# A delta-rule attention layer and two MLPs on one core: the second triangular solve, the K Kᵀ products of chunks 4 and 5 and the loads of chunk 2 take other places in chunks 0 to 3

## The chip, the cores and the metric

The kernel is one program on one core of a Trainium2 chip. The metric is the device time of one execution in microseconds (us). Engines are named as in the profile: PE is TensorE (matmuls), PEld its weight load, DVE is VectorE, ACT is ScalarE, POOL is GpSimd, SP is SyncE, which here only issues DMAs. L454 is line 454 of the kernel before. In the changed kernel the lines behind 364 are two higher, those behind 900 about as much again, and the text says which one is meant where it matters.

## The reference, cut to what matters

```
def _attn_ref(q, k, v, beta):                       # 4 x 8 heads, 768 steps, 48 features
    k_n = k / (np.linalg.norm(k, axis=-1, keepdims=True) + 1e-06)
    for t in range(S):
        y[:, :, t] = einsum('bhd,bhde->bhe', q[:, :, t], state)
        v_old = einsum('bhde,bhd->bhe', state, k_n[:, :, t])
        state = state + beta[:, :, t] * outer(k_n[:, :, t], v[:, :, t] - v_old)

x = y as (3072 tokens, 384)
h = np.maximum(x @ w_in, 0.0);  x = h * h @ w_out                         # 384 -> 2048 -> 384
h = max(x @ w1, x @ w2, x @ w3);  out = h @ w_out2                         # 384 -> 768 -> 384
```

All of it is float32. The kernel splits each float32 operand of the large matmuls in a high and a low part and adds three products.

## The kernel before, in words

**Chunks.** The 768 steps are cut into 12 chunks of 64. Inside a chunk the recurrence is a triangular system, so per chunk the kernel needs three things that do not depend on the state: the products K Kᵀ and K Qᵀ of all 32 heads (`kkps`, matmuls at L180, copied out by ACT at L197 and masked by DVE at L198, and stored to DRAM by `kk_store` and L205), the inverse of the triangular matrix (`solve32`), and the loads of keys, values and inverse (`load_x`, `load_att`). The chunks are handled in pairs, `HALVED[g]` being chunks 2g and 2g+1.

**The solve.** `solve32(g)` inverts for both chunks of a pair at once. `start32` loads the blocks of K Kᵀ into `M32` (a piece of the tile `buf`). `ready` (`prep`, `weighted`, `strict`, L217 to L238) turns them into a scaled triangular matrix, and `solve` (L278) does 30 elimination steps of two dependent DVE instructions each (a product at L283, a sum at L285), which grow from 30 to 240 columns and shrink again, and then one scaling of 1024 columns (L286). `finish32` stores the inverse to `xt_d` (L323). `load_x(c)` reads it back as `xb` (L342) and `x1` (L350), together with a block of K Kᵀ, `k21` (L339).

**Attention of a chunk.** `attention(c)` is a generator of seven stages: `st0` (L436 to L449: scales `v`, multiplies keys and queries with the state `Sb` into `pA` and `pY`, and subtracts `pA` from `v`), `zz` (`merged`: DVE transposes `x1` into `xT` at L404, PE makes `pZ` at L411, ACT copies it out at L412), `ww` (PE makes `pW` at L420 from `xT` and the copy, ACT copies it into `xb`), `mm_u` (`pU`, L464), `st2` (`pY` and `pD`, L514 and L492, and the new state, L499), `st3` (transposes at L532 into the high and low parts `xh` and `xl`, L535 and L536). All these small products share one PSUM pool of two buffers, `ps_at`: `pk`, `pq`, `pA`, `pZ`, `pW`, `pU`, `pD`, `pt` and `pT` take turns in it, and each waits until the one two before it has been read.

**The MLP of a chunk.** `moe_a(c)` multiplies the 256 tokens of a chunk with `w_in` (L572, 18 matmuls per piece `s1`), squares the positive part on ACT (L578 to L580, `gh`), makes the low part `gl` on DVE (L581), and multiplies with `w_out` into `px` (L592, 12 matmuls per piece `s2`, two pieces behind). At its end DVE transposes `px` (L612). There are 8 pieces of each kind in a chunk. In chunk 1 (`halves`) every piece is cut into two steps.

**What sets the order.** While chunk c's MLP runs, `steps` calls other generators in between: `attention(c+1)`, the solve of a later pair, the K Kᵀ of a pair, and in chunk 0 the rest of the weight words (`weights`, `words`, `turn`: L103 to L128). A list of numbers says after which step of the MLP a generator goes one yield further, `True` behind it that what is left over stays for later. The instructions of an engine run in the order in which they were recorded, except that the scheduler moves some, DMA issues above all, ahead. `behind` (L269) orders an instruction after another. In chunk 0 the last word loads of `w_out` (L93) go out on SP, and the keys of chunk 2 (`kq`, L364) on POOL.

**The schedule of before around the change** (L895 to L931). The second solve (pair 1: chunks 2 and 3) does 10 yields in chunk 0 and the rest in the first part of chunk 1. The K Kᵀ of chunks 4 and 5 stands in steps 14 to 24 of chunk 1, between the stages of `attention(2)`. The third solve (pair 2) runs through chunk 2.

Of the kernel before, what the change touches and what calls it, by code (L numbers as in the profile page):

```python
# [39 lines left out]
def delta_moe(ctx, tc, kc, ab, kt, vt, beta, beta32, beta16, kq, w_in, w_out, w1, w2, w3, w_out2, out):  # L40
    nc = tc.nc
# [117 lines left out]
    def two(d, c, p):  # L159

        return d[:, c, 2 * p:2 * p + 2]
# [196 lines left out]
    def load_att(c, p):  # L358
        ds = []
        us = slice(U2 * p, U2 * p + U2)  # L360
        kq_ = None
        if c:
            kq_ = att.tile([R2, U2, 2, C], F32, name="kq", tag="kq")
            ds.append(pool.dma_start(kq_, two(kc, c, p).rearrange("p b q t s -> p (b q) t s")))  # L364
        v = att.tile([128, U2, D], F32, name="v", tag="v")
        ds.append(pool.dma_start(v, two(vt, c, p).rearrange("p b q d -> p (b q) d")))
        pt_ = masked.pop((c, p), None)
        if pt_ is None:
            pt_ = att.tile([128, U2, C], F32, name="p", tag="p")
            ds.append(pool.dma_start(pt_, p_d[c][:, us]))  # L370
        kt_ = ktp[p]
        ds.append(pool.dma_start(kt_[:, 0:U2 * D], two(kt, c, p).rearrange("p b q d -> p (b q d)")))
        for i in x_after:
            for d in ds:
                behind(d.ins, i)
        tiles[c, p] = [kq_, v, xb[:, us], pt_, kt_, None, None, None, None]
# [5 lines left out]
    def attention(c):  # L382
# [158 lines left out]
        both = lambda f: ((f, 0), (f, 1))  # L541
        if c:
            order = ((load, 0),), both(st0), ((merged, 0),), *(((),) if c == 1 else ()), ((ww, 0),), both(mm_u), both(st2), both(st3)
            if c == 2:
                order = order[1], order[0], *order[2:]
        else:
            load(0)
            load_att(c, 0)
            load_att(c, 1)
            order = both(st0), ((merged, 0),), ((ww, 0),), both(mm_u), both(st2), both(st3), both(state)  # L550
# [154 lines left out]
    if True:  # L705
# [19 lines left out]
        def solve32(g, load=(nc.sync, nc.sync), store=((nc.sync,) * 2,) * 2, landing=0):  # L725
# [9 lines left out]
            for n, i in enumerate(solve(vec, M, 32, 64 * len(HALVED[g]), a, tmp32)):  # L735
                for j in solve_after:
                    behind(i.ins, j)
                ops.append(i.ins)
                if g and n == (24 if g == 1 else 8):
                    norm(nm)  # L740
                yield
            finish32(g, M, store)
# [152 lines left out]
        for c in range(NC):  # L895
            extra = []
            if c == 0:
                solve_next = solve32(1, (pool,) * 2)
                extra += [(11 / 15.0, later(3, attention(1))), (list(range(17)), weights(2, 2)), (4.0, later(20, part(solve_next, 10)))]
            elif c == 1:  # L900
                pinned.update({first_matmul.ins.engine: None, last_gl[0].engine: None})
                first_solve = [0] * 3 + [1 + n * 13 // 20 for n in range(20)]
                extra += [(first_solve, solve_next), ([15, 17, 24, 26, 28, 30, 31], attention(2))]
                ahead_[2] = solve32(2, landing=1)
                extra += [([14, 15, 19, 20, 21, 22, 23, 24], kkps(HALVED[2], (at,))), ([26, 32], ahead_[2], True)]
                solve_after[:] = last_vec
                kc_after[:] = raws[-1:]
                prep_after.clear()
            elif c + 1 < NC:
                extra.append(([1, 2, 5 + c // 9, 7 + c // 9, 10, 12, 14] if c % 2 else [1, 2, 4, 6, 8, 11, 13], attention(c + 1)))  # L910
            if c == 2:
                kc_after.clear()
                solve_after.clear()
            if c in ahead_:
                extra.append(([1 + n * 14 // 32 for n in range(32)], ahead_[c]))
            if c > 1 and c in KK:
                extra.append(([3, 4, 4, 5, 6, 7, 8, 9], kkps(HALVED[KK[c]], (at,))))
# [128 lines left out]
```

## Time and profile before

| | before |
|---|---|
| median of 3 runs | 926.25 us (925.52 to 926.77) |
| the profiled execution | 926.38 us, its span 924.4 us |
| PE busy | 868.5 us (94%) |
| DVE busy | 475.8 us (51%) |
| ACT, POOL busy | 376.0 us (41%), 146.6 us (16%) |
| DMA | 98.82 MB, mean 107 GB/s |

The profiled execution takes 2 us more than its span, which is what lies before the first and behind the last instruction. PE is busy nearly all the time, but a share of 94% is a mean: in the slices of the page the first eighth of the span has PE at half and the clock of TensorE below its full value, and from the tenth of the span on there are nines. So the stages must be read apart: where the long chains begin and end, what PE waits for in each, and how fast its clock ran there. A wait of PE is told with what ended it; where the profile says "issue", PE waited for nothing that it shows.

### The profile page before, as it was taken

What the parts mean: (1) busy time and instruction counts of PE and PEld (TensorE: products, weight loads), DVE (VectorE), ACT (ScalarE), POOL (GpSimd) and SP (SyncE); (2) the same over time, 40 slices, a digit from 0 to 9 for tenths busy, and PEclk for the clock granted to TensorE, in tenths of its full rate; (3) what the DMA queues carried; (4) which work ended last, traced back from release to release, by engine and by line L of the source; (5) the groups of instructions that cost most, each with busy time, mean ns of one, the idle gap of its engine ahead of it and who ended that gap; (6) DMA issues with size and microseconds to landing.
All of it is one profiled execution on the core that took longest, in us unless ns stands there. A gap on an engine that the chain in (4) does not pass through costs nothing.

```text
span 924.4 us, 26481 instructions
## 1 busy us (share of the span) xinstructions
PE 868.5 (94%) x11422; PEld 843.0 (91%) x11422; DVE 475.8 (51%) x1068; ACT 376.0 (41%) x799; POOL 146.6 (16%) x241
## 2 busy tenths in 40 slices
PE   5439899899999999999999999999999999999998
PEld 5328888799999999999999999999999999999998
DVE  2978886288348734873586364457232322323221
ACT  1447853353445344544453556564121221212111
POOL 2323121411331133122313300002000000000000
PEclk8557999899999999999999999999999999999999
DMA  9987634732852284337434551334110101000000
GB/s 196 309 256 226 202 83 133 194 96 67 207 160 66 85 215 133 78 87 190 104 82 104 143 146 53 102 107 136 38 37 31 35 18 43 10 26 9 18 18 35
DMA packets 122596, 98.82 MB, mean 107 GB/s; under 512 B 77440, under 2 KB 102832, under 8 KB 122480
## 3 DMA queue, kind: packets, MB, share of 16 engines
q1 hardware_dynamic: 101824, 58.42, 24.1%
q0 software_dynamic: 11584, 32.22, 12.2%
q10 hardware_dynamic: 9072, 6.49, 2.4%
q8 instruction: 90, 1.47, 0.7%
q14 instruction: 26, 0.21, 0.1%
HBM read 72.45 MB, written 24.64 MB: 105 GB/s over the span
## 4 chain that ended last, share of the span: by engine, by line
PE 84%; DVE 8%; DMA 3%; ACT 2%; issue 1%; ACTq 0%; SPq 0%; DVEq 0%
PE p L954 24%; PE px L592 21%; PE p L572 20%; PE po L971 8%; PE pY L514 2%; PE pU L464 2%; DVE buf L283 2%; DVE buf L285 2%; PE pk L180 1%; PE pW L420 1%; DMA kct<-in_kc_dram 1%; PE pZ L411 1%; PE pA L445 1%; DMA raw<-in_moe_w_out_dram 1%; DVE gl L581 1%
## 5 line engine op out<-in xcount | busy, mean ns | idle before, releaser
L954 PE MATMUL p<-x_h,w 128*128 128x384 f32 x864 | 220.1, 336 | 0.0
L592 PE MATMUL px<-wout,gh 128*128 128x384 f32 x768 | 200.6, 342 | 0.4 <-ACT gh L580 0.4
L572 PE MATMUL p<-xh,win_h 128*128 128x256 f32 x576 | 169.6, 294 | 2.0 <-DVE gl L581 1.4
L572 PE MATMUL p<-xl,win_h 128*128 128x256 f32 x576 | 164.0, 285 | 0.3 <-DVE xl L536 0.3
L572 PE MATMUL p<-xh,win_l 128*128 128x256 f32 x576 | 164.0, 285 | 0.0
L954 PEld LDWEIGHTS p<-x_h,w 128*128 128x128 f32 x864 | 156.2, 188 | 0.0
L954 PE MATMUL p<-x_l,w 128*128 128x384 f32 x432 | 145.2, 336 | 0.0
L581 DVE TENSOR_TENSOR gl<-p,gh 128x512 fp32r<-128x512 f32 x96 | 66.2, 690 | 144.8 <-ACT gh L580 144.5
L592 PEld LDWEIGHTS px<-wout,gh 128*128 128x128 f32 x768 | 135.6, 190 | 1.9 <-ACT gh L580 0.6
L592 PE MATMUL px<-wout,gl 128*128 128x384 f32 x384 | 129.6, 337 | 0.0
L578 ACT ACTIVATE p<-p 128x512 f32<-128x512 f32 x96 | 55.9, 582 | 176.0 <-PE p L572 176.0
L572 PEld LDWEIGHTS p<-xh,win_h 128*128 128x128 f32 x576 | 111.0, 193 | 5.3 <-DVE gl L581 1.9
L572 PEld LDWEIGHTS p<-xl,win_h 128*128 128x128 f32 x576 | 111.1, 193 | 0.6 <-DVE xl L536 0.5
L572 PEld LDWEIGHTS p<-xh,win_l 128*128 128x128 f32 x576 | 111.4, 193 | 0.0
L960 DVE TENSOR_TENSOR mx<-p,mx 128x384 f32<-128x384 f32 x48 | 26.7, 557 | 126.7 <-PE p L954 126.6
L954 PEld LDWEIGHTS p<-x_l,w 128*128 128x128 f32 x432 | 81.2, 188 | 0.0
L962 ACT CAST hh<-mx 128x384 fp32r<-128x384 f32 x48 | 24.6, 513 | 125.8 <-DVE mx L961 125.8
L592 PEld LDWEIGHTS px<-wout,gl 128*128 128x128 f32 x384 | 72.7, 189 | 0.0
L285 DVE TENSOR_TENSOR buf<-buf 128x30 f32<-128x30 f32 (+9 forms) x180 | 61.1, 339 | 6.1
L283 DVE TENSOR_TENSOR buf<-buf 128x30 f32<-128x30 f32 (+9 forms) x180 | 60.6, 337 | 5.0
L580 ACT CAST gh<-p 128x512 fp32r<-128x512 f32 x96 | 56.4, 587 | 2.6
L579 ACT ACTIVATE p<-p 128x512 f32<-128x512 f32 x96 | 55.9, 583 | 2.6
(166 smaller groups left out, 1290.7 us busy)
## 6 DMA issues: line engine op xcount, KB each, us to landing
kq<-in_kc_dram POOLq DMA_DIRECT2D x22, 448.0 KB, 5.3
raw<-in_moe_w_dram SPq DMA_DIRECT2D x18, 384.0 KB, 3.5
raw<-in_moe_w_out_dram SPq DMA_DIRECT2D x16, 384.0 KB, 4.4
p<-p POOLq DMA_DIRECT2D x22, 256.0 KB, 3.6
rawp<-in_moe_w_in_dram SPq DMA_DIRECT2D x12, 384.0 KB, 10.3
v<-in_vt_dram POOLq DMA_DIRECT2D x24, 192.0 KB, 3.0
ktp<-in_kt_dram POOLq DMA_DIRECT2D x24, 192.0 KB, 3.6
x<-xs SPq DMA_DIRECT2D x48, 96.0 KB, 3.2
```

The lines of the kernel that those rows point to most:

```text
L283: eng.tensor_tensor(out=tv, in0=M[:, 0:j, j].unsqueeze(2).broadcast_to([u, j, m]), in1=M[:, j, j + 1:n].unsqueeze(1).broadcast_to([u, j, m ...
L285: yield eng.tensor_tensor(out=M[:, 0:j, j + 1:n], in0=M[:, 0:j, j + 1:n], in1=tv, op=ALU.add)
L572: pe.matmul(p1[:, j], w[:, k, f], x[c][:, k], start=n == 0 and j == 0, stop=n == 8, skip_group_check=True)
L578: act.activation(out=p1, in_=p1, func=AF.Relu)
L579: act.activation(out=p1, in_=p1, func=AF.Square)
L580: last_gh[0] = act.copy(gh, p1).ins
L581: last_gl[0] = vec.tensor_sub(out=gl, in0=p1, in1=gh.bitcast(F32)).ins
L592: g = pe.matmul(px[:, h, 0:DM], x[:, j, hs], w, start=f == 0 and i == 0, stop=f == NF - 1 and i == 2, skip_group_check=True)
L954: pe.matmul(p, w[i][:, k, fs], x[:, k], start=n == 0, stop=n == 8)
L960: vec.tensor_max(out=t, in0=ps[1], in1=t)
L962: act.copy(hh[:, f], t2)
L971: pe.matmul(po[:, 0:DM], x[:, f, js], w[:, f], start=i == 0, stop=i == 17)
```

## The change

- The keys of chunk 2 (`kq`) are loaded on SP's queue instead of POOL's, ordered behind the last word load of `w_out`.
- `attention(4)` starts with `st0` and then loads its inverse, as `attention(2)` did already. The norms of pair 2 are made after 4 solve steps instead of 8.
- The second solve does one yield at step 4 of chunk 0 (its preparation) and 14 at steps 7 to 16, and has 18 yields left for chunk 1. Its store for chunk 2 goes half on SP and half on POOL.
- In chunk 1, `attention(2)` has its places one or two half steps later, and the K Kᵀ of chunks 4 and 5 stands at steps 27 to 32, the end of the chunk.
- The third solve does 28 yields in chunk 2 (the last 26 from step 5 on) and 6 at the start of chunk 3. `attention(4)` has later places in chunk 3.

```diff
@@ load_att
         if c:
             kq_ = att.tile([R2, U2, 2, C], F32, name="kq", tag="kq")
-            ds.append(pool.dma_start(kq_, two(kc, c, p).rearrange("p b q t s -> p (b q) t s")))
+            ds.append((nc.sync if c == 2 else pool).dma_start(kq_, two(kc, c, p).rearrange("p b q t s -> p (b q) t s")))
+            if c == 2:
+                behind(ds[-1].ins, raws[-1])
@@ attention
-            if c == 2:
+            if c in (2, 4):
                 order = order[1], order[0], *order[2:]
@@ solve32
-                if g and n == (24 if g == 1 else 8):
+                if g and n == {1: 24, 2: 4}.get(g, 8):
                     norm(nm)
@@ the loop over the chunks
             if c == 0:
-                solve_next = solve32(1, (pool,) * 2)
-                extra += [(11 / 15.0, later(3, attention(1))), (list(range(17)), weights(2, 2)), (4.0, later(20, part(solve_next, 10)))]
+                solve_next = solve32(1, (pool,) * 2, ((nc.sync, pool), (nc.sync,) * 2))
+                extra += [(11 / 15.0, later(3, attention(1))), (list(range(17)), weights(2, 2)), ([4] + [7 + n * 10 // 14 for n in range(14)], solve_next, True)]
             elif c == 1:
                 pinned.update({first_matmul.ins.engine: None, last_gl[0].engine: None})
-                first_solve = [0] * 3 + [1 + n * 13 // 20 for n in range(20)]
-                extra += [(first_solve, solve_next), ([15, 17, 24, 26, 28, 30, 31], attention(2))]
+                first_solve = [0] * 3 + [1 + n * 11 // 15 for n in range(15)]
+                extra += [(first_solve, solve_next), ([16, 17, 24, 26, 28, 30, 32], attention(2))]
+                extra += [([27, 28, 29, 30, 31, 32, 32, 32], kkps(HALVED[2], (at,)))]
                 ahead_[2] = solve32(2, landing=1)
-                extra += [([14, 15, 19, 20, 21, 22, 23, 24], kkps(HALVED[2], (at,))), ([26, 32], ahead_[2], True)]
...
             elif c + 1 < NC:
-                extra.append(([1, 2, 5 + c // 9, 7 + c // 9, 10, 12, 14] if c % 2 else [1, 2, 4, 6, 8, 11, 13], attention(c + 1)))
+                places = [2, 4, 7, 8, 10, 12, 14] if c == 3 else [1, 2, 5 + c // 9, 7 + c // 9, 10, 12, 14] if c % 2 else [1, 2, 4, 6, 8, 11, 13]
+                extra.append((places, attention(c + 1)))
...
-            if c in ahead_:
+            if c == 2:
+                extra.append(([1, 4] + [5 + n * 12 // 26 for n in range(26)], ahead_[c], True))
+            elif c == 3:
+                extra.append(([0, 1, 1, 2, 2, 2], ahead_[2]))
+            elif c in ahead_:
                 extra.append(([1 + n * 14 // 32 for n in range(32)], ahead_[c]))
```

What this does to the order, at three places. First SP's queue in chunk 0 (`raw` are word loads of `w_out`, `kq` and the loads into `buf` and `big` are keys), before:

```order
L93 DMA buf<-in_moe_w_out_dram 128x768
L93 DMA raw<-in_moe_w_out_dram 128x768 x4
L167 DMA buf<-in_kc_dram 112x1024
L167 DMA big<-in_kc_dram 112x1024
L299 DMA b_2366<-in_beta_dram 64x32 x2
```

and now:

```order
L93 DMA raw<-in_moe_w_out_dram 128x768 x4
L364 DMA kq<-in_kc_dram 112x1024
L167 DMA buf<-in_kc_dram 112x1024
L364 DMA kq<-in_kc_dram 112x1024
L167 DMA big<-in_kc_dram 112x1024
L299 DMA b_2591<-in_beta_dram 64x32 x2
```

The four word loads now have four key loads behind them on one queue, where there were two, with two more on POOL's queue.

Second, DVE at the end of chunk 0, from the steps of the second solve to the low part `xl` that chunk 1's first matmuls read, before:

```order
L285 TENSOR_TENSOR buf<-buf 128x9x22
L283 TENSOR_TENSOR buf<-buf 128x210
L499 TENSOR_TENSOR Sb<-pD,Sb 128x384 x2
L612 STREAM_TRANSPOSE xs<-px 128x384 x2
L536 TENSOR_TENSOR xl<-pT,xh 128x3x128 x2
```

and now (L501, L614 and L538 are L499, L612 and L536 of before):

```order
L285 TENSOR_TENSOR buf<-buf 128x12x19
L501 TENSOR_TENSOR Sb<-pD,Sb 128x384
L283 TENSOR_TENSOR buf<-buf 128x234
L285 TENSOR_TENSOR buf<-buf 128x13x18
L283 TENSOR_TENSOR buf<-buf 128x238
L285 TENSOR_TENSOR buf<-buf 128x14x17
L283 TENSOR_TENSOR buf<-buf 128x240
L501 TENSOR_TENSOR Sb<-pD,Sb 128x384
L614 STREAM_TRANSPOSE xs<-px 128x384 x2
L538 TENSOR_TENSOR xl<-pT,xh 128x3x128 x2
```

Ten more solve instructions (from the sum with 10x21 columns to the product with 240) stand ahead of the transposes, five of them between the two updates of the state `Sb`, which free the two PSUM buffers that the transposes at L532 need.

Third, DVE in chunk 1, from the end of the second solve (L286) to the end of the chunk (`pq` is one K Qᵀ block each), before:

```order
L286 TENSOR_TENSOR buf<-buf,a_1183 128x1024
L581 TENSOR_TENSOR gl<-p_1902,gh 128x512
L198 TENSOR_TENSOR buf<-pq,mask 128x512
L436 TENSOR_TENSOR v<-v,normT 128x384
L449 TENSOR_TENSOR v<-v,pA 128x384
L436 TENSOR_TENSOR v<-v,normT 128x384
L449 TENSOR_TENSOR v<-v,pA 128x384
L581 TENSOR_TENSOR gl<-p_2059,gh 128x512
L198 TENSOR_TENSOR big<-pq,mask 128x512
L198 TENSOR_TENSOR buf<-pq,mask 128x512
L581 TENSOR_TENSOR gl<-p_2149,gh 128x512
L198 TENSOR_TENSOR big<-pq,mask 128x512
```

and now, from the transposition `xT` on, which in before stands behind the last of these rows:

```order
L406 STREAM_TRANSPOSE xT<-x_2028 128x256
L583 TENSOR_TENSOR gl<-p_2139,gh 128x512
L198 TENSOR_TENSOR buf<-pq,mask 128x512
L476 COPY u<-pU 128x288
L476 COPY u<-pY 64x96 x2
L198 TENSOR_TENSOR big<-pq,mask 128x512
L501 TENSOR_TENSOR Sb<-pD,Sb 128x384 x2
L526 COPY yy<-pY 64x4x48 x4
L198 TENSOR_TENSOR buf<-pq,mask 128x512
L614 STREAM_TRANSPOSE xs<-px 128x384 x2
L538 TENSOR_TENSOR xl<-pT,xh 128x3x128 x2
L198 TENSOR_TENSOR big<-pq,mask 128x512
```

The four K Kᵀ blocks of PE moved along: they stood ahead of `pZ`, and now stand one each between `pW`, `pU`, `pY`/`pD`, `pT` and the first matmuls of chunk 2.

## Rows read from the trace of the kernel before

**Rows 1.** The page, part 2: TensorE's clock in 40 slices, tenths of full.
```profile
PEclk8557999899999999999999999999999999999999
```

**Rows 2.** The chain that ended last: start us, length us, what.
```profile
129.63 0.92 DVE xl L536 x2
130.59 2.19 PE p L572 x16
...
230.03 4.32 PE p L572 x36
...
278.27 4.30 PE p L572 x36
...
320.48 4.32 PE p L572 x36
```

**Rows 3.** Timeline of PE, first main matmul of chunk 2: start us, length us.
```profile
187.04 0.28 PE L572 MATMUL p<-xh,win_h 128*128 128x256 f32 x1
```

**Rows 4.** PE's waits in chunk 0, then chunks 1 and 2: us, times, longest us.
```profile
PE pZ L411 <- DVE v L449: 3.1, 1, 3.1
...
PE pW L420 <- issue: 3.0, 1, 3.0
PE pA L445 <- DVE buf L198: 1.1, 1, 1.1
PE p L572 <- DVE gl L581: 0.9, 2, 0.5
PE pT L532 <- DVE yy L524: 0.7, 1, 0.7
```

**Rows 5.** Windows behind two waits: us, engines' busy us (count), PEclk, DMA share, GB/s.
```profile
172.40:177.40 5.00, 4.96 (x43) 4.46 (x45) 0.69 (x1) 2.04 (x5) 1.29 (x2) 0.50 0.71 201
109.20:113.00 3.80, 3.75 (x77) 3.68 (x78) 3.80 (x10) 3.26 (x7) 0.00 (x0) 0.58 0.03 13
```

**Rows 6.** DVE's timeline, chunk 0's end to chunk 3: start us, length, [idle before, ended by].
```profile
108.38 0.36 DVE L116 TENSOR_SCALAR raw<-raw 128x384 int32<-128x384 int32 x1 [2.12 <-DMA raw<-in_moe_w_out_dram]
...
128.58 1.05 DVE L612 STREAM_TRANSPOSE xs<-px 128x384 f32<-128x384 f32 x2 [2.41 <-PE px L592]
...
130.46 0.35 DVE L285 TENSOR_TENSOR buf<-buf 128x210 f32<-128x210 f32 x1
...
133.87 0.41 DVE L285 TENSOR_TENSOR buf<-buf 128x238 f32<-128x238 f32 x1
...
148.57 1.22 DVE L286 TENSOR_TENSOR buf<-buf,a 128x1024 f32<-128x1024 f32 x1
...
188.21 0.15 DVE L247 COPY ss<-buf 128x32 f32<-128x32 f32 x1
...
228.20 1.22 DVE L286 TENSOR_TENSOR buf<-buf,a 128x1024 f32<-128x1024 f32 x1
...
234.07 0.69 DVE L581 TENSOR_TENSOR gl<-p,gh 128x512 fp32r<-128x512 f32 x1 [2.95 <-ACT gh L580]
```

**Rows 7.** Timelines of POOL and SP: DMA issues, start us, length us.
```profile
99.29 0.55 POOL L364 DMA_DIRECT2D kq<-in_kc_dram  x1 [2.90 <-PE pY L445]
...
100.09 0.33 SPq L93 DMA_DIRECT2D raw<-in_moe_w_out_dram  x1
...
158.25 0.66 POOL L342 DMA_DIRECT2D xb<-xt  x1 [0.70 <-issue]
```

**Rows 8.** DMA issues of 95 to 101 us: KB each, median us to landing.
```profile
raw<-in_moe_w_out_dram SPq DMA_DIRECT2D x4, 384.0 KB, 5.6
...
big<-in_kc_dram SPq DMA_DIRECT2D x1, 448.0 KB, 9.9
```

**Rows 9.** DMA issues of 100 to 190 us.
```profile
xb<-xt POOLq DMA_DIRECT2D x6, 64.0 KB, 3.2
```

**Rows 10.** DMA queues of 170 to 171 us: packets, MB, share of 16 engines.
```profile
q8 instruction: 1, 0.02, 6.0%
```

**Rows 11.** The chain of 90 to 200 us: start us, length us.
```profile
100.09 8.27 DMA raw<-in_moe_w_out_dram
```

## The prediction, made before the changed kernel was run

> **What bounds the kernel now.** I read the clock line first: from the tenth slice of 23 us on it is full, so what can be won lies in the first quarter [rows 1]. Then the chain of waits, for the places where PE begins 36 main matmuls in a row: these are chunk starts. Chunk 1's main matmuls run from 130.59 us behind the DVE part `xl`, chunk 3 starts at 230.03, chunk 4 at 278.27, chunk 5 at 320.48 [rows 2]; chunk 2, from the timeline, at 187.04 [rows 3]. So chunk 1 takes 56.45 us, chunk 2 42.99, chunk 3 48.24 and chunk 4 42.21. An odd chunk holds the K Kᵀ of a pair, an even one does not, so chunk 3 and chunk 4 are the measure: chunk 1 is 8.2 us too long, chunk 2 0.8.
>
> PE's waits name most of it: in chunk 1, 3.0 before `pW` for nothing that the profile shows, 1.1 before `pA` for a masked block, 0.7 before `pT`, and one of 0.5 before a main piece, 5.3 together; in chunk 0, 3.1 before `pZ` [rows 4]. Each of the two long ones has a tail: the five us behind the first ran at clock 0.50, the 3.8 behind the second at 0.58 [rows 5], where the 1.1 before `pA` left the clock full. The lower level is 1.2 of 2.4 GHz, so the first tail lost 2.5 us and the second 1.6.
>
> What held `pZ` in chunk 0: `pZ` takes the PSUM buffer of `pA`, which DVE frees by the subtraction L449; DVE stood 2.12 us in front of a word operation until 108.38 [rows 6], because the last word load, issued at 100.09 [rows 7], took 8.27 us [rows 11]. Key loads were around it, on POOL's queue from 99.29 [rows 7] and on SP's behind it, the last of which took 9.9 [rows 8].
>
> **The change part by part.** The work of PE is the same, so I sum what each chunk start moves.
>
> *Chunk 0, -0.6.* In before DVE goes from 108.38 to the end of `xl` at 130.55 (129.63 + 0.92) in 22.17 us, of which 2.41 wait for PE's last `px` [rows 2, 6]: 19.76 of work. Ten solve instructions come on top; nine of them took from 130.46 to 134.28 in before [rows 6], so ten cost 4.2. Five short preparation steps move ahead of the landing and one word operation behind it; these I count as equal. That is 24.0 us from the landing to `xl`. The word load now goes out some 0.3 later, behind two short operations, and has all four key loads behind it instead of one ahead and two behind. I take the median of the four word loads, 5.6 us [rows 8]: landing at 106.0, `xl` at 130.0, against 130.55. Bounds: DVE itself cannot be there before about 105.5 (108.38 less its 2.12 of idle, less what it waits for earlier word loads), so -1.1; if the word load takes the longest of these loads, 9.9, it lands at 110.3 and the term is +3.7. The point is that DVE, not PE, now ends chunk 0: what PE gains at `pZ` is hidden.
>
> The Trainium skill ("DMA: Bandwidth & Descriptors", section "Queues, rings and completion order") says that each DMA engine takes the descriptors of one ring in order and goes round robin between rings. By that the four key loads on the same ring cannot delay the words, and the term is -1.1. The trace agrees only in part: with two key loads behind it on its own queue and one beside it the word load took 8.27 us.
>
> *Clock behind it, +1.6.* PE does not wait long at `pZ` any more: DVE passes two word operations, one reciprocal and the subtraction, some 2 us, behind the landing, so `pZ` starts near 108.1, and PE comes there 0.8 later than before, having seven more main matmuls of 0.12 us (4.32 for 36) to do first. Without the tail of 1.6 us PE ends its `px` some 3.6 us earlier, about 125, and the second buffer for `pT` comes free 2 us before `xl` ends, about 128. So a wait of 3 us goes from `pZ` to the end of the chunk. The two rows with a 3 us wait both show a fall of the clock, the 1.1 us one does not [rows 4, 5]; I take the fall, with the price of the shorter tail. Bounds 0 and 2.5.
>
> *Chunk 1, -5.9.* Here the solve has 16 steps left instead of 21, so its scaling, 18.0 us behind the chunk's start in before (148.57 [rows 6]), comes four to five us earlier, and the inverse goes out on two queues. `attention(2)` runs without the K Kᵀ between `st0` and `pZ`. The wait before `pA` goes, since no block of K Kᵀ holds the PSUM in front of it. The 3.0 before `pW`: PE stopped within the 64 matmuls of `pW`, with its operands there, and in that time the queue "instruction" moved one packet of 0.02 MB [rows 10]. So PE waited for its own code, behind the loads of K Kᵀ for the third solve and the stores. Now `pW` has only main pieces ahead of it and no store of K Kᵀ beside it; I take this wait and its tail as gone. The 0.5 before a main piece stays, being a matter of ACT and DVE behind the first piece. At the chunk's end PE finds no `px` to do between `pT` and the next chunk as it did in before: the fourth K Kᵀ block needs both PSUM buffers of `pT`, read by `xl`, which stands behind two transposes of `px`: 1.05 and 0.92 us [rows 2, 6] less six small transposes of 0.1 each, 1.4. Sum: 56.45 - 5.3 - 2.5 + 0.5 + 1.4 = 50.55. Bounds: 48.2, chunk 3's length, and 56.45 if the code waits elsewhere.
>
> *Chunk 2, -0.5.* Its order on PE stays; it had 0.8 us over chunk 4. Its solve starts later: in before the first copy of `ss` came 1.2 us into the chunk (188.21 [rows 6]), now behind `xT`, some 11 us into it, since the last K Kᵀ block is stored only at the chunk's start. This costs DVE, not PE. Bounds -0.8 and +1.5.
>
> *Chunk 3, +1.2.* The solve took from 188.21 to 229.4, 41 us, most of it DVE's own work [rows 6]; 10 us later it ends some 10 to 11 us into chunk 3. The last six yields stand there in front of and around the subtraction that the first K Kᵀ block waits for. DVE had 2.95 us of idle there [rows 6], which covers most of the five steps before it; I count 0.5. The last load of the inverse was issued 8.5 us behind the end of the scaling in chunk 1 (149.79 to 158.25 [rows 6, 7]) and takes 3.2 us [rows 9], 11.7 in all; PE reaches `pZ` some 11 us behind the scaling now: 0.7. Bounds 0 and 3.4, the 2.95 uncovered and more.
>
> Later chunks keep their order. Sum: -0.6 + 1.6 - 5.9 - 0.5 + 1.2 = -4.2. The profiled execution took 926.38, which is 0.13 above the median; so 922.2 against it, and 922.0 as a median.
>
> **The rivals.** *Better (918.8).* The words land as early as DVE can take them and the clock holds: -1.1, 0, -5.9, -0.7, +0.3. For it: `pT`'s first three transposes break the idle stretch. Against it: both waits of 3 us.
>
> *One wait for code moves (925 to 927.5).* From `pW` on, chunk 1 now has some 480 small and `px` matmuls in about 15 us, denser than before, and stores and loads that were spread from 150 to 187 us fall together there. One wait like that of before is 3.0, or 5.5 with its tail.
>
> The Trainium skill ("Runtime: NRT & Kernel Launch", section "Instruction fetch mechanics") says that code comes in blocks of 16 KiB over a DMA queue of its own, fetched ahead, and that the cost of a block's border is mostly hidden. One packet of 0.02 MB fits such a block. By the rule this rival has no place; the trace shows one wait where it was not hidden.
>
> *Slower (933).* The same mechanism twice: between `pW` and the first pieces of chunk 2 two blocks of code land later than PE uses up the block before, which here takes it about 4 us. It decides if the DMA engines are as full there as at 172 to 177, share 0.71 [rows 5], and fuller. Price 2 x 5.5 on 922.0. Against it: before had one such wait in the whole stretch.
>
> *It does not do what it says (928).* The inverse of chunk 2 is read back late, on two queues that hold other work, so `pZ` and `pW` wait as long as `pW` did: the -5.9 is lost.
>
> **How the numbers follow.** Forecast 0.47, for itself 920 to 924; better 0.20; one wait for code 0.18; slower 0.10; not as said 0.05. About 0.2%, 1.85 us, is what a measurement can tell from no change, so faster means below 924.4 and slower above 928.1. Faster: 0.46 + 0.20 + a third of 0.18, 0.72. Same: 0.01 + 0.12 + 0.03, 0.16. Slower: 0.10 and 0.02 of the last, 0.12. The range goes from 918.0, which leaves out a small part of the better case, to 927.5, which leaves out the slower one and some of the last: 918.0 to 927.5.
>
> **What would show it.** Chunk 0: the wait before `pZ` at 1 us or less, a wait of 2 to 3 us before `pT` ended by DVE's `Sb` or solve, the start of chunk 1 near 130 and a half clock behind it. Chunk 1: no wait within `pW`, none for L198 before `pA`, chunk 2 from 179 to 183. Chunk 3: a wait of 0.5 to 1 us for `v` at the first K Kᵀ block, and about as much at `pZ` for `xb`. I am wrong if "issue" stands among PE's waits of 155 to 185 us, if chunk 1 starts behind 132, or if the saving is not in chunk 1.

## The result, and the profile after

| | before | changed |
|---|---|---|
| median of 8 runs each | 925.88 us (921.58 to 928.20) | 932.85 us (928.78 to 937.14) |
| the profiled execution, its span | 926.38, 924.4 us | 930.66, 928.8 us |

The ratio is 1.0067, with a 95% interval of 1.0043 to 1.0092: the change makes the kernel slower by some 6 us. The forecast was 922.0 (918.0 to 927.5), a gain of 4 us; the kernel lost time instead, and its median lies above the range. The profiled execution of the changed kernel is one of its faster ones; what follows accounts for the 4.4 us between the two spans.

The chain of waits of the changed kernel (start us, length us, what), the rows that answer to [rows 2, 3, 11]:

```profile
100.84 4.82 DMA raw<-in_moe_w_out_dram
...
128.77 2.19 PE p L574 x16
...
174.26 3.41 issue
...
184.53 4.51 PE p L574 x36
...
238.27 2.44 DMA xt<-buf
...
244.91 6.70 DMA xb<-xt
...
252.60 3.84 PE px L594 x12
...
259.99 3.68 PE p L574 x18
...
282.76 4.30 PE p L574 x36
...
324.97 4.32 PE p L574 x36
```

The chunk starts give the whole account of the two spans. Chunk 1 starts at 128.77 (130.59 before), chunk 2 at 184.53 (187.04), chunk 4 at 282.76 (278.27), chunk 5 at 324.97 (320.48). So the changed kernel is 1.8 us ahead at chunk 1, 2.5 ahead at chunk 2, and 4.5 behind at chunk 4; from there nothing changes any more. Chunk 3, whose first main matmul stands at 226.99 on the timeline, lasts 55.6 us instead of 48.2. In this execution that stretch alone turns a small gain into the loss. It is a long one: in the four kernels below with the same places and the same late inverse in chunk 3 (experiments 2, 4, 5 and 6) it lasts 52.6 to 53.3 us, so 4.4 to 5.1 of the 7.4 us repeat.

PE's waits from 76 to 290 us (total, times, longest), to be held against [rows 4]:

```profile
PE pk L180 <- issue: 3.4, 1, 3.4
PE pZ L413 <- DMA xb<-xt: 2.5, 1, 2.5
PE pT L534 <- DVE Sb L501: 1.9, 1, 1.9
PE pq L180 <- ACT xb L429: 1.8, 2, 1.3
PE pk L180 <- DVE xl L538: 0.9, 1, 0.9
...
PE pq L180 <- DVE v L451: 0.6, 1, 0.6
...
PE pZ L413 <- DVE v L451: 0.5, 1, 0.5
```

The 3.1 before `pZ` for `v` has shrunk to 0.5, and the 1.1 before `pA` is gone, as forecast. The wait that the profile cannot name is still there, now before a K Kᵀ block and 0.4 us longer. New are the 2.5 for `xb` and a 1.3 for ACT behind it, both in chunk 3.

The windows (us, busy us of PE, PEld, DVE, ACT, POOL, then PEclk, DMA share, GB/s), as in [rows 5]:

```profile
120.00:140.00 20.00, 16.86 (x182) 15.92 (x174) 18.07 (x46) 9.22 (x23) 2.16 (x4) 1.00 0.28 73
170.00:180.00 10.00, 6.59 (x205) 5.83 (x204) 3.33 (x8) 1.84 (x5) 2.65 (x5) 0.88 0.91 258
240.00:250.00 10.00, 9.14 (x177) 8.47 (x176) 2.08 (x3) 3.63 (x7) 4.90 (x8) 1.00 0.95 239
250.00:260.00 10.00, 6.93 (x205) 6.31 (x205) 1.04 (x2) 2.92 (x8) 3.59 (x6) 0.81 0.70 186
260.00:270.00 10.00, 10.00 (x117) 9.70 (x118) 2.35 (x5) 3.99 (x10) 2.20 (x4) 0.85 0.72 177
```

The granted clock stays full over the end of chunk 0, and falls behind the wait in chunk 1 and behind the two in chunk 3. In the chain the price of the last fall is seen directly: 12 `px` matmuls take 3.84 instead of 2.1 to 2.3 us, and 18 main matmuls 3.68 instead of 2.35. With the three waits (2.5, 1.3, and 0.3 more for `v`) that is some 7 of the 7.4 us.

DVE's timeline at three places that answer to [rows 6]:

```profile
105.68 0.36 DVE L116 TENSOR_SCALAR raw<-raw 128x384 int32<-128x384 int32 x1 [0.65 <-DMA raw<-in_moe_w_out_dram]
...
198.66 0.19 DVE L247 COPY ss<-buf 128x32 f32<-128x32 f32 x1 [2.33 <-DMA buf<-kk]
...
237.02 1.23 DVE L286 TENSOR_TENSOR buf<-buf,a 128x1024 f32<-128x1024 f32 x1
```

The last words land 2.7 us earlier. The third solve starts at 198.66 instead of 188.21, because its input leaves PE only at the end of chunk 1, and so its scaling ends at 238.25, some 11 us into chunk 3, instead of just ahead of it. PE came to `pZ` at 249.2; the last two parts of `xb` were issued from 244.91 on, behind other loads of the inverse on POOL's queue, and the one that the chain names took 6.70 us with the DMA engines 0.95 busy.

### The profile page after: what moved, and what is told of

Same layout as the page of the kernel before. It is cut to its first block, busy times and chain, and to the rows that moved or that the text cites. A ratio compares the mean times of both kernels' runs of the same rounds, so it can differ in the third digit from the quotient of the medians.

```text
span 928.8 us, 26472 instructions
## 1 busy us (share of the span) xinstructions
PE 869.2 (94%) x11422; PEld 843.6 (91%) x11422; DVE 475.5 (51%) x1068; ACT 376.1 (40%) x799; POOL 146.0 (16%) x240
## 4 chain that ended last, share of the span: by engine, by line
PE 80%; DVE 9%; DMA 5%; ACT 3%; issue 2%; POOL 0%; SPq 0%; ACTq 0%; DVEq 0%; POOLq 0%
PE p L961 24%; PE p L574 19%; PE px L594 19%; PE po L978 8%; DVE buf L283 2%; DVE buf L285 2%; PE pY L516 2%; PE pU L466 2%; PE pA L447 1%; DMA xb<-xt 1%; DMA kct<-in_kc_dram 1%; PE pk L180 1%; DVE gl L583 1%; PE pZ L413 1%; PE pW L422 1%
## 5 line engine op out<-in xcount | busy, mean ns | idle before, releaser
L580 ACT ACTIVATE p<-p 128x512 f32<-128x512 f32 x96 | 55.9, 583 | 174.5 <-PE p L574 174.3
L582 ACT CAST gh<-p 128x512 fp32r<-128x512 f32 x96 | 56.4, 587 | 2.7
```

Source lines behind the costliest of these rows:

```text
L580: act.activation(out=p1, in_=p1, func=AF.Relu)
L582: last_gh[0] = act.copy(gh, p1).ins
```

## The experiments

Each kernel is compared with runs of the kernel before on the same chip; ratios have a 95% interval. Lines of kernels built on the changed one, and of the ninth, are two higher, as before. Medians come from several chips, so kernels are best compared by their ratios. Starts and lengths of chunks are from PE's timeline of the profiled execution, in us; chunk 1 starts with its first matmul with `xl`, chunks 2 and 3 with their first main matmul. Behind chunk 3, where no order changes, the profiled executions take 646.1 to 648.4 us to the end, so differences of 2 us between single executions mean little.

| kernel | median | ratio to before | chunk 1 starts | chunk 1 | chunk 2 | chunk 3 |
|---|---|---|---|---|---|---|
| before | 925.9 | | 130.6 | 56.4 | 42.8 | 48.2 |
| changed | 932.85 | 1.0067 (1.0043 to 1.0092) | 128.8 | 55.7 | 42.5 | 55.6 |
| 1 K Kᵀ back | 923.84 | 0.9985 (0.9961 to 1.0008) | 126.5 | 56.5 | 42.8 | 48.7 |
| 2 K Kᵀ alone | 932.13 | 1.0081 (1.0051 to 1.0110) | 130.7 | 57.3 | 44.5 | 52.6 |
| 3 `pZ` later | 930.47 | 1.0060 (1.0034 to 1.0085) | 127.9 | 56.8 | 44.2 | 52.9 |
| 4 64 more warm-up matmuls | 958.58 | 1.0369 (1.0315 to 1.0422) | 154.1 | 55.4 | 44.1 | 52.8 |
| 5 less traffic | 929.62 | 1.0060 (1.0038 to 1.0081) | 127.6 | 57.0 | 42.4 | 53.3 |
| 6 one warm-up matmul | 931.08 | 1.0079 (1.0054 to 1.0104) | 127.4 | 54.1 | 43.5 | 52.8 |
| 7 solve cut | 926.67 | 1.0026 (1.0008 to 1.0043) | 128.7 | 55.8 | 45.6 | 51.7 |
| 8 K Kᵀ in the middle | 918.65 | 0.9944 (0.9921 to 0.9967) | 128.5 | 50.4 | 43.4 | 48.0 |
| 9 key loads alone | 920.26 | 0.9937 (0.9915 to 0.9958) | 125.3 | 53.8 | 43.0 | 48.7 |
| 10 second solve alone | 929.93 | 1.0038 (1.0020 to 1.0056) | 132.2 | 57.8 | 42.8 | 48.1 |
| 11 middle alone | 933.34 | 1.0072 (1.0047 to 1.0096) | 131.5 | 60.3 | 43.4 | 48.0 |
| 12 middle, 12 steps | 918.58 | 0.9917 (0.9897 to 0.9938) | 125.8 | 50.7 | 43.4 | 48.1 |

**1 and 2: the two halves of the change.** The first undoes K Kᵀ, the third solve and `attention(4)` in the changed kernel, the second does these alone in the kernel before.

```diff
-([16, 17, 24, 26, 28, 30, 32], attention(2)), ([27, 28, 29, 30, 31, 32, 32, 32], kkps(HALVED[2], (at,)))
+([15, 17, 24, 26, 28, 30, 31], attention(2)), ([14, 15, 19, 20, 21, 22, 23, 24], kkps(HALVED[2], (at,))), ([26, 32], ahead_[2], True)
...                                    # and the third solve and attention(4) as before; the second kernel is the reverse
```

> The changed kernel with K K^T of chunks 4 and 5, the third solve and attention(4) back where the kernel before has them; chunk 0's 14 solve steps, the two store queues and the key load on SP stay. Theory: of the loss, +7.4 us are chunk 3 (waits of 2.5 before pZ and 1.3 behind pW, 0.6 before the first K K^T, and a fall of the clock) and come from the late third solve; chunk 0 gives back 1.8. So chunk 3 lasts about 48.2 us again, chunk 1 starts near 128.8, and the time is 922 to 925. Rival: chunk 0's gain is only run to run, or is handed on to chunk 1 as a wait; then the time is 926 to 928. Rival: the loss in chunk 3 comes from the stores on two queues; then it stays above 930.

> The kernel before with only the other part of the change: K K^T of chunks 4 and 5 at the end of chunk 1, the third solve in chunks 2 and 3, attention(4) at its new places. Chunk 0, the second solve and its stores are those of the kernel before. Theory: this part alone carries the loss: chunk 3 some 55 us instead of 48.2, a wait of 2 to 3 us before pZ for xb, a wait for nothing that the profile shows within chunk 1's end; time 932 to 936. Rival (the loss needs the second solve's stores on two queues, which delay the third's loads): 926 to 928.

The first lands where the theory had it, 923.84, though it can't be told from the kernel before; chunk 3 is back at 48.7. The second has all of the loss, 1.0081. So the loss belongs to K Kᵀ and the third solve with the new places of `attention(2)` and `attention(4)`, and the second solve's stores have no part in it. Two pieces of the second's chain, and then its wait for the inverse, show both costs without any help from chunk 0. The wait is shorter than the 2 to 3 us that were expected, and chunk 3, at 52.6, shorter than the 55:

```profile
176.84 3.03 issue
...
250.50 5.47 DMA xb<-xt
```

```profile
PE pZ L411 <- DMA xb<-xt: 1.1, 1, 1.1
```

**3 and 7: what costs in chunk 3.** One lets PE come later to `pZ`, the other lets the inverse come earlier.

```diff
# 3
-                places = [2, 4, 7, 8, 10, 12, 14] if c == 3 else ...
+                places = [2, 4, 9, 10, 11, 13, 14] if c == 3 else ...
# 7: steps 27 to 30 of the third solve left out, the rest ends with chunk 2
-            elif c == 3:
-                extra.append(([0, 1, 1, 2, 2, 2], ahead_[2]))
```

> The changed kernel with attention(4)'s pZ and pW two places later in chunk 3, behind the last block of K K^T. Theory: chunk 3's loss is the wait for the inverse and what follows it: PE reaches pZ at 252 or later, where xb has landed (251.6); the 2.5 and the 1.3 go and the clock does not fall, some 6 us less: 926 to 928. Rival: the loss is DVE's, which runs behind through the first half of chunk 3 whatever PE does, and the waits come back before pU or pY: 930 to 934.

> The changed kernel with the last four of the 30 elimination steps of the third solve left out, so that the solve and the store of its inverse end with chunk 2 (chunks 4 and 5 are computed from an unfinished inverse). PE's order is the same. Theory: chunk 3's loss comes from the time at which the third solve ends: xb lands before PE is at pZ, the wait of 2.5 and the clock's fall go, the 1.3 behind pW stays, being a matter of order; chunk 3 lasts 49 to 51 us instead of 55.6, time 926.5 to 929. Rival: PE's new order in chunk 3 (pW straight ahead of a K K^T block) or the traffic of chunk 3's own K K^T is what costs; chunk 3 stays above 53 and the time above 930.

The third is a miss: the wait for `xb` is gone, but one of 1.9 for ACT's `u` and one of 0.4 come in its place further on, the clock falls behind the first, and chunk 3 keeps 52.9 us. That is its rival, 930 to 934. Its windows (columns as above) put the loss behind the place where it stood before:

```profile
246.00:256.00 10.00, 10.00 (x182) 9.37 (x182) 2.77 (x4) 4.18 (x8) 1.64 (x3) 1.00 0.82 194
256.00:282.00 26.00, 23.37 (x429) 22.18 (x428) 9.36 (x23) 10.59 (x26) 10.85 (x17) 0.93 0.58 157
```

The seventh brings the median to 926.67, as the theory said, and PE no longer waits for `xb`. But chunk 3, at 51.7 us, is longer than the 49 to 51 expected and still 3.5 us longer than in the kernel before: PE waits 1.45 behind `pW`, where a K Kᵀ block now follows at once and needs the PSUM that ACT is reading, and the clock falls there too:

```profile
250.00:260.00 10.00, 8.18 (x221) 7.31 (x220) 1.57 (x4) 4.02 (x10) 3.59 (x6) 0.90 0.81 210
260.00:270.00 10.00, 10.00 (x122) 9.70 (x122) 2.10 (x5) 4.49 (x12) 3.04 (x5) 0.93 0.67 176
```

So 3.5 us stay with the new order of `attention(4)` among the K Kᵀ blocks. What goes with the late inverse is less certain: 3.9 us against the 55.6 of the changed kernel's profile, but only 0.9 to 1.6 against the 52.6 to 53.3 of experiments 2, 4, 5 and 6. By the ratios, 1.0026 and 1.0067, it is some 3.8 us, each ratio being good to some 2 us. (The profiled execution of the seventh, 930.07, is the slowest of its twelve runs; its chunk 2 is 3 us longer, since PE waits 1.4 us there for `nm`, which DVE now makes between the steps of the cut solve, and the clock falls behind it.)

**4, 5 and 6: the wait that the profile does not name.** The prediction took it for PE's wait for its own code, and then took it as gone.

```diff
# 4
+        for _ in range(64):
+            pe.matmul(pw[:, 0, 0:16], warm, warm[:, 0:16], start=True, stop=True)
# 6
-        NWARM = 8
+        NWARM = 1
# 5, for c == 3
-            ds.append(pool.dma_start(pt_, p_d[c][:, us]))
+            ds.append(pool.memset(pt_, 0.0) if c == 3 else pool.dma_start(pt_, p_d[c][:, us]))
+        n = D if c == 3 else U2 * D          # columns of kt_ that are loaded
```

> The changed kernel with 64 small extra matmuls in PE's warm-up at the start, so that all of PE's code behind them stands 64 matmuls further on. Theory: the 3.4 us before the third K K^T block of chunk 1, for nothing that the profile shows, are PE's wait for a block of its own code, and stand where such a block ends (behind 2377 matmuls in the changed kernel): the wait then comes 64 matmuls earlier in the order, within pY and pD, or goes; the time stays within 2 us of the changed kernel, or falls by 4 to 6. Rival: PE waits for something that this K K^T block needs (a load, a buffer): the wait stays at the block's 17th matmul.

> The changed kernel without the loads of P and with a sixth to a quarter of the keys of chunk 3 that are issued at 171.9 to 174.1 us (P is filled with zeros instead; what chunk 3 computes from them is left out). Theory: before the third K K^T block PE waits for a packet of its own code, which in the changed kernel moves only at 175 to 176 us because the DMA engines are full (share 0.99); with some 0.8 MB less around it the packet moves earlier, the wait of 3.4 us falls below 1.5, and the time to 928 to 930. Rival: the small matmuls use the code up faster than it can come, whatever else is on the DMA engines: the wait stays at 3 us or more, and the time at 931 to 934.

> The changed kernel with 1 instead of 8 matmuls in PE's warm-up. The experiment with 64 more warm-up matmuls left the wait at the 17th matmul of the third K K^T block; but an fp32 matmul shows as two in the trace, each with a weight load, so that 64 are 256 instructions, as many as lie between one packet of code and the next, and moved nothing. Seven fewer are 14 matmuls of the trace. Theory (a block border of PE's code): the wait comes 14 matmuls later in the order, at the 31st of the block. Rival (something that this block needs): it stays at the 17th. Time within 2 us of the changed kernel by either.

The matmuls of the third K Kᵀ block (L180) ahead of the wait and behind it, in the windows of that line alone (PE's busy us and count first). First the changed kernel, then the fourth, then the sixth:

```profile
173.70:174.40 0.70, 0.50 (x17) 0.42 (x18) 1.00 1.01 307
177.60:179.25 1.65, 1.56 (x47) 1.37 (x46) 0.52 0.67 154
```

```profile
200.10:200.80 0.70, 0.50 (x17) 0.42 (x18) 1.00 1.04 214
202.60:203.80 1.20, 0.93 (x47) 0.78 (x46) 1.00 1.01 395
```

```profile
172.40:173.20 0.80, 0.69 (x31) 0.56 (x32) 1.00 0.95 338
174.80:175.60 0.80, 0.70 (x33) 0.56 (x32) 1.00 1.01 390
```

With 64 matmuls more the wait stays behind the 17th, as its rival had it; taken alone this would speak for something that the block needs. (Its time, 958.58, is another matter: these matmuls delay the prologue, and chunk 0's first long run of main matmuls, by 24 us; from there to the end the two profiled executions take the same 849.5.) With 7 matmuls less it comes behind the 31st: 14 later, exactly as many as the trace shows for 7. Nothing else about that block has changed. So the wait hangs on the place in PE's code and not on the work. A place that repeats after 256 instructions, 64 fp32 matmuls at two matmuls and two weight loads each, explains the fourth kernel too. That is also what the page gives: 90 packets of the queue "instruction" for PE's 22,844 matmuls and weight loads, 254 per packet. And it holds in every kernel: ahead of such a wait of over 1 us in chunk 1 the traces count 4546 instructions of PE (in the kernel before and in 1, 9 and 10, where it stands within `pW`), 4801 (in the changed kernel and in 2, 3, 5, 6 and 7) or 5057 (in 4), 255 and 256 apart.

The traces also show what ends it and what sets its length. In the changed kernel one packet of the queue "instruction" moves between 175 and 176 us, and none from 168.5 to 175 (columns as in [rows 10]):

```profile
q8 instruction: 1, 0.02, 6.8%
```

In all eleven kernels PE goes on 1.2 to 1.5 us behind the end of such a packet. The packet starts from 2.3 us before PE stops (experiment 9, a wait of 1.3) to 1.0 behind it (experiment 5, a wait of 3.3): the wait is as long as the packet is late.

The fifth says what does not shorten it. Here 0.9 MB less is moved, and the wait is as long as ever, though the median, 929.62, is where the theory had it:

```profile
PE pk L180 <- issue: 3.3, 1, 3.3
```

The windows of that stretch and, for the fifth, of the one ahead of it, the fifth kernel's and then the changed kernel's:

```profile
170.00:174.00 4.00, 3.90 (x153) 3.40 (x152) 2.20 (x6) 1.25 (x4) 2.24 (x5) 1.00 0.95 219
174.00:178.00 4.00, 0.78 (x29) 0.78 (x32) 0.33 (x1) 0.00 (x0) 0.00 (x0) 0.79 0.38 128
```

```profile
174.00:178.00 4.00, 0.59 (x30) 0.51 (x26) 0.71 (x2) 0.00 (x0) 0.15 (x1) 0.96 0.92 334
```

With a DMA share of 0.38 during the wait instead of 0.92, it takes 3.3 instead of 3.4. Ahead of the wait, though, the engines were as full as before, 0.95, so the fifth does not clear the traffic there. The rival, that PE uses its code up too fast, fits: from 160.3 to 174.3 us the changed kernel runs some 400 small matmuls with only 30 `px` between them. But speed alone does not bring the wait. Two stretches of 256 of PE's instructions in the changed kernel, cut where the wait can stand; no wait follows the first, the 3.4 us follow the second:

```profile
157.33:160.73 3.40, 3.40 (x133) 3.23 (x135) 0.86 (x2) 0.71 (x2) 2.25 (x4) 1.00 0.07 19
170.85:174.05 3.20, 3.20 (x143) 2.90 (x136) 1.87 (x5) 1.26 (x4) 2.11 (x4) 1.00 0.92 242
```

They differ in the DMA share, 0.07 and 0.92, and in the stretch ahead of each, which took 9.8 and 4.7 us. Cut so, the last stretch ahead of the wait takes 3.2 to 3.7 us in all eleven kernels, at a DMA share of 0.91 or more, and no stretch of chunk 1 takes less than 4.6 us in experiments 8, 11 and 12, which have no such wait. So in chunk 1 dense small matmuls and full DMA engines stand together wherever PE waits, and no experiment parts the two.

**9 and 10: the parts of chunk 0.**

```diff
# 9, in the kernel before
-            ds.append(pool.dma_start(kq_, ...))
+            ds.append((nc.sync if c == 2 else pool).dma_start(kq_, ...))
+            if c == 2:
+                behind(ds[-1].ins, raws[-1])
# 10, in the kernel before
-                ... (4.0, later(20, part(solve_next, 10)))
+                ... ([4] + [7 + n * 10 // 14 for n in range(14)], solve_next, True)
-                first_solve = [0] * 3 + [1 + n * 13 // 20 for n in range(20)]
+                first_solve = [0] * 3 + [1 + n * 11 // 15 for n in range(15)]
```

> The kernel before with the key loads of chunk 2 on SP's queue behind the last word load, and nothing else of the change. Theory: this alone brings the last word load in at 105.5 to 106 us (in the kernel before 108.4, in the changed kernel 105.7) and takes away most of the 3.1 us before pZ; DVE has less to do in chunk 0 here, so that PE ends it and chunk 1 starts at 127 to 128.5, against 130.6. Chunk 1 stays at 56 to 57 us. 922.5 to 924, that is 2 us under the kernel before. Rival: the word load is late because of the key loads behind it on SP, which are more now: chunk 1 starts at 130 to 131, no change.

> The kernel before with 14 of the second solve's steps in chunk 0 and its stores on two queues, the key loads still on POOL. Theory: the words land as in the kernel before (108.4) and DVE has 4.2 us more to do behind them, which its 2.4 us of idle at the chunk's end does not cover: chunk 1 starts at 132 to 133; chunk 1 with K K^T at its old places is 56 to 58 us, as in the first experiment (57.2), so that nothing comes back: 926 to 928. Rival: the earlier inverse shortens chunk 1 by 2 us or more: 923 to 925.

The ninth is the surprise: these three lines alone take 5.8 us off (0.9937 of 926.0), more than the theory had. PE's first main matmul with `xl`, with the wait ahead of it, and its two longest waits behind 76 us:

```profile
125.30 0.39 PE L574 MATMUL p<-xl,win_h 128*128 128x256 f32 x1 [0.27 <-DVE xl L538]
```

```profile
PE pW L422 <- issue: 1.3, 1, 1.3
PE pA L447 <- DVE buf L198: 1.1, 1, 1.1
```

No wait before `pZ` is left in chunk 0, and chunk 0, from its first long run of main matmuls, is 46.8 us long instead of 51.45: 4.65, which is the wait of 3.1 and the tail of 1.6 together. Chunk 1 gains 2.6 more, since the code wait within `pW` is 1.3 here instead of 3.0 and the clock does not fall behind it. The tenth is 2 us worse than its theory, though its chunks 0 and 1 are as long as expected; in the profiled execution the 2 us lie behind chunk 3 and are unexplained. The word load is late as in the kernel before, PE waits 3.6, and the earlier inverse buys nothing in chunk 1, where a key load for K Kᵀ now comes late (2.3). Its chain and its waits:

```profile
100.23 8.52 DMA raw<-in_moe_w_out_dram
```

```profile
PE pZ L411 <- DVE v L449: 3.6, 1, 3.6
PE pk L180 <- DMA buf<-in_kc_dram: 2.3, 1, 2.3
```

**8, 11 and 12: K Kᵀ in the middle.** The eighth keeps the change's chunk 0, spreads K Kᵀ over the middle of chunk 1, and lets the third solve end with chunk 2.

```diff
# 8, in the changed kernel; chunk 3 as before
-([16, 17, 24, 26, 28, 30, 32], attention(2)), ([27, 28, 29, 30, 31, 32, 32, 32], kkps(HALVED[2], (at,)))
+([15, 17, 20, 23, 26, 29, 31], attention(2)), ([18, 19, 21, 22, 24, 25, 27, 28], kkps(HALVED[2], (at,))), ([30], ahead_[2], True)
...
-                extra.append(([1, 4] + [5 + n * 12 // 26 for n in range(26)], ahead_[c], True))
+                extra.append(([2] + [3 + n * 13 // 32 for n in range(32)], ahead_[c]))
# 11: 8 with the second solve, its stores and kq of the kernel before
# 12: 8 with 12 solve steps in chunk 0, and the last K Kᵀ block at 28, 29
```

> The changed kernel with the blocks of K K^T of chunks 4 and 5 in the middle of chunk 1 (places 18, 21, 24, 27 instead of 27, 29, 31, 32; in the kernel before 14, 19, 21, 23), each between parts of attention(2), which stand at 15, 17, 20, 23, 26, 29, 31; the third solve's landing at place 30, its preparation at the third place of chunk 2, all its steps in chunk 2; chunk 3 as in the kernel before. Theory: chunk 0 keeps its gain of 2 us or more, the third solve ends with chunk 2, so that chunk 3 lasts 48 to 49, and the small matmuls and the transfers lie further apart, so that chunk 1 lasts 52 to 55: 919 to 923. Rival: the transfers still collide and one wait for code or for a key load with its tail stays in chunk 1: 924 to 927.

> The kernel with K K^T in the middle of chunk 1, without the change's part in chunk 0: second solve, its stores and the key loads are those of the kernel before. Theory: chunk 1 needs the inverse of chunk 2 early (pZ at place 20), and here it comes 4 to 5 us later, so that PE waits at pZ for 1 to 4 us: chunk 1 lasts 52 to 55 instead of 50.4, chunk 0 ends at 130.6: 921 to 925. Rival: where K K^T stands is all that counts, the solve has slack: chunk 1 at 50 to 51 and 919.5 to 921, 2 us above the version with all of chunk 0's part.

> The kernel with K K^T in the middle of chunk 1, with 12 instead of 14 of the second solve's steps in chunk 0 and the last K K^T block one place later. Theory: DVE ends chunk 0 (2.0 us of wait before pT, and 0.6 and 0.2 behind it); two steps less are four instructions of 0.41 us, so chunk 1 starts 1.6 us earlier, at 127, and the inverse still lands before pZ; the 0.7 before the last K K^T goes: 916 to 918. Rival: the steps come back in chunk 1 as a wait at pZ or pW: 918 to 920.

The eighth is at 918.65, with chunk 1 at 50.4 us and no wait for code in it, both better than expected. The eleventh is far worse than expected: without the earlier second solve PE stands before `pZ` for 6.4 us. The profile gives no releaser, but the last part of `xb` is issued only then; it does not fit a wait for code, since it stands at another place, behind 3834 instructions, and the last packet of code ended 7.3 us before PE went on. Its chain, and POOL's timeline:

```profile
157.10 6.39 issue
```

```profile
157.83 0.66 POOL L342 DMA_DIRECT2D xb<-xt  x1 [0.73 <-issue]
```

With the 3.1 us that these loads take there it lands near 160.9; the 2.6 us from there to `pZ` at 163.49 stay unexplained. So the order of K Kᵀ pays only with chunk 0's part of the change; that the earlier end of the second solve is what counts in it is argued, not shown, since the eleventh also has the key loads of the kernel before. The twelfth starts chunk 1 almost 3 us earlier than the eighth and gives 1.7 of it back at `pZ`, which is its rival:

```profile
PE pZ L413 <- DMA xb<-xt: 1.7, 1, 1.7
```

Its median, 918.58, is within the eighth's runs, so the two can't be told apart. With 0.9944 and 0.9917 both beat the kernel before, by 5 and 8 us, and the changed one by 11 and 14. The windows of the twelfth show where the clock now stays full, from chunk 0's end into chunk 2, with the DMA engines 0.91 busy over the last 30 us:

```profile
120.00:130.00 10.00, 9.11 (x63) 8.53 (x62) 9.20 (x23) 4.07 (x10) 1.33 (x3) 1.00 0.52 133
130.00:150.00 20.00, 19.53 (x307) 18.85 (x307) 14.38 (x37) 9.55 (x20) 4.09 (x7) 1.00 0.37 72
150.00:180.00 30.00, 28.27 (x639) 25.89 (x638) 10.47 (x21) 11.16 (x26) 9.57 (x16) 1.00 0.91 228
```

## Why the prediction was wrong, step by step

The sum was -4.2; measured by the same chunk starts it is +4.5. Two steps failed, and they make up more than the difference.

*"Chunk 1, -5.9 ... I take this wait and its tail as gone."* Measured: -0.8. The wait before `pA` and the one before `pT` did go. The code wait did not: it hangs on a border in PE's code (experiment 6), the change only moved which work stands there, and the small matmuls around it became denser. It is 3.41 us, with a tail of 1.7, half of the 3.4 us at half clock:

```profile
177.65:181.05 3.40, 3.38 (x53) 3.26 (x53) 0.69 (x1) 0.59 (x1) 0.00 (x0) 0.50 0.77 131
```

With it in, the step's own sum of 50.55 gives 55.7; measured 55.7. The rival "one wait for code moves" described this correctly, at 925 to 927.5, and had 0.18. The rival "slower" names almost the measured median, 933, but by luck: it asked for two such waits, there is one, and the rest came from chunk 3. The prediction's own sign of being wrong, "issue" among PE's waits of 155 to 185 us, stands in the chain at 174.26. That the 50.55 was a fair size for a chunk 1 without the wait is shown by experiments 8 and 12, with 50.4 and 50.7.

*"Chunk 3, +1.2. Bounds 0 and 3.4."* Measured: +7.4. The mechanism was in the text, the size was not. The end of the solve some 11 us into the chunk and PE's arrival 11 us behind it were right. The last part of the inverse was issued even earlier than forecast, 6.7 us behind the scaling instead of 8.5. But its load was priced at the 3.2 us of [rows 9], taken from chunk 1, where in chunk 3 it took 6.70, with the loads and stores of K Kᵀ beside it on full DMA engines; the wait got no tail, though two waits in [rows 5] had one; and the step looked only at when the inverse comes and not at what the new places put behind `pW`. Experiment 7 leaves 3.5 us for the order; the 3.9 for the inverse holds for the profiled execution and is 0.9 to 1.6 against the 52.6 to 53.3 us of other kernels. Even those exceed the bound of 3.4, which did not carry the tail.

*"Chunk 0, -0.6" and "clock behind it, +1.6".* Together +1.0, measured -1.8. The landing was forecast for 106.0 and came at 105.66. From there DVE took 23.0 us to the end of `xl` instead of 24.0. PE does wait at the chunk's end (1.9 before `pT`, 0.6 and 0.2 behind it), but the clock held in this execution, as the rival "better" had it. It is no rule: in experiment 1, where the chunk ends alike, the granted clock was 0.91 over 120 to 140 us. That DVE ends chunk 0 and hides what PE gains was right, and it hides more than was thought: the key loads alone are worth 4.65 us in chunk 0, and with the ten solve instructions of the change 2.7 of them are gone.

The Trainium skill ("DMA: Bandwidth & Descriptors", section "Queues, rings and completion order") says that a DMA engine takes the descriptors of one ring in order; by that the key loads behind the words on one queue cost them nothing. The runs agree in the main: with all four key loads behind it on SP the word load takes 4.82 us, with two of them on POOL's queue 8.27 before and 8.52 in experiment 10. That the cost is nothing is not shown, for the three word loads ahead of it took 3.2 to 3.8.

The Trainium skill ("Runtime: NRT & Kernel Launch", section "Instruction fetch mechanics") gives 256 instructions for a block of code and calls the cost of a block's border mostly hidden. The runs agree with the first, 256 instructions from one place of the wait to the next, and not with the second: 3.41 us here.

*"Chunk 2, -0.5".* Measured -0.3.

The sum of the measured terms, -1.8 - 0.8 - 0.3 + 7.4, is +4.5. The medians differ by 7.0; the rest has no place in the two profiled executions, of which that of the changed kernel lies 2.2 below its median.

## What to carry to other kernels

When a change shifts the end of a long chain on a side engine, price the first consumer with the load's time in the stretch where it will now run, the clock behind the wait, and what else the consumer's new place pushes together; and let the upper bound carry all of that. A wait that the profile cannot name does not go away because other work stands there now; move the code by a few instructions, and if the wait moves by as many, it is a wait for code. Spreading the small products among the large matmuls removed it here. Run the parts of a bundled change one by one: here three lines alone gained 5.8 us, and the rest covered it.

## What the runs showed of the hardware

- PE waits at borders in its own code that repeat after 256 instructions. Waits of this kind, of 1.1 to 3.4 us, stand in chunk 1 of eleven of the fourteen kernels, and end 1.2 to 1.5 us behind a packet of the queue "instruction". In each of the eleven the last 256 of PE's instructions ahead of the border took 3.2 to 3.7 us, with the DMA engines 0.91 or more busy; a stretch as fast at a share of 0.07 had no wait behind it, and a DMA share of 0.38 instead of 0.92 during the wait did not shorten it. What makes the packet late was not settled.
- With key loads of 448 KB just ahead of it on POOL's queue a word load on SP's queue took 8.3 to 8.8 us (four kernels); with the same loads behind it on SP's own queue it took 4.0 to 5.5 (the eight kernels of ten whose trace tells it).
- A fall of the granted clock to half can cost much of the wait ahead of it once more: in chunk 3 of the changed kernel 2.9 us behind waits of 3.8. The three kernels that beat the kernel before by 5 us or more (8, 9 and 12) are the three with a granted clock of 1.00 over 100 to 290 us; in the others it was 0.95 to 0.98.
